# Loading and splitting two weights of the last product earlier, in tiles that the attention's projections leave free

## The chip, the core and the metric

The kernel runs on one core of a Trainium2 chip. Its time is the device time of that core in microseconds; the value given is the median of 3 runs.

The engines are called as the profile calls them: PE (TensorE, matrix products), DVE (VectorE), ACT (ScalarE), POOL (GpSimd) and SP (SyncE, which here only issues transfers). Transfers are issued from two queues, SP's and ACT's. Each queue issues in order, and each transfer takes its turn among eight completion semaphores, so that it may wait for an older transfer with the same semaphore to land.

## The reference

Three stages run one after the other. What matters here is the last part of the second and the whole of the third.

```python
# stage 1: linear attention over phi(q), phi(k), v            (8 x 8 heads x 576 x 64)
# stage 2: mixture of E=4 causal attention experts            (8 x 576 x 512)
for e in range(E):
    q = x @ wq[e]; k = x @ wk[e]; v = x @ wv[e]
    scores = where(causal, -1e9, scale * (q @ k.T))
    a = softmax(scores)
    out += gate[e] * (a @ v @ wo[e])
# stage 3: token mix and gated feed-forward                   (d_model 512, d_ff 1024)
x_prev = concat([0, x[:, :-1]])
xk = mu_k * x + (1 - mu_k) * x_prev
xr = mu_r * x + (1 - mu_r) * x_prev
k = maximum(xk @ w_k, 0.0)
v = k * k @ w_v
r = 1.0 / (1.0 + exp(-(xr @ w_r)))
return r * v
```

## The kernel before

All products are float32 made of pieces: each operand is split in a high half (a rounded copy, written by ACT, L97) and a low half (the rest, `src - hi`, by DVE or POOL, L100), and a product is hi·hi + hi·lo + lo·hi, three matmuls.

**Stage 2** goes through batches b = 0 to 7. `qk` are the projections with the weights `wqh, wql, wkh, wkl` (tiles of 128 x 1024 in pool `pQ`, made at the start, read until the last batch's projections), `sc` the scores (L514, L515), `a` the exponentials (ACT, L534; scaled on POOL, L545), `at` their transposes (L552, split to `at1h`/`ath` on ACT L568 and `at1l`/`atl` on DVE L569), `yp` the product with v (L587). After the last `yp` of a batch half, `yf` and its time differences `dl` are split to `yt` and stored to DRAM as `yd` (SP, L608).

**Stage 3, first product (`rk`).** `gates_keys` computes x @ w_r and x @ w_k, for both taps, for 6 chunks of tokens. A unit is 6 matmuls of 128x384; its weight `wt` (256 KB) comes by ACT's queue, 5 buffers deep. DVE adds three partial results into `z` (L720), ACT squares the keys' ones (Relu L722, Square L723), and SP's queue stores `z` to DRAM as `kd` (L724).

**Stage 3, last product (`vacc`, L882).** `moe2` computes k² @ w_v in seven products per chunk (a Strassen scheme over 2x2 blocks): operands b11, b21, T2, T1, b22, T3, T4 in this order (j = 0 to 6), with weights `WC[0, 1, 3, 4, 5, 6, 2]`, 24 matmuls of 128x384 each. The blocks of the squared keys come back from `kd` by SP's queue, are combined on DVE (L845 to L858) and split into slots of the tile `XT`, which before that held stage 2's activations. The results are evacuated as `t` (ACT) and `o` (DVE, L906, L915). `zs` are the gate's inputs r (two loads of 768 KB per chunk, L822; a table load and the sigmoid on ACT, L835).

Stage 2's attention and the `rk` units of the later chunks run woven together; the `rk` units fill PE while the attention's softmax runs elsewhere. At the attention's end (about 1009.7 us) follows the first chunk of the last product. Its first block b11 comes as two half loads `k0` (L794), the other three (b21, b12, b22) straight into parts of `XT` that are free (L797); b21 is split there (L97, `XT<-XT`). `first()` writes this part, `chunk(0)` the rest.

Of the seven weights, four (0, 1, 3, 4) are loaded and split in the attention's middle (`combo`, two halves of 128x512, low half on POOL). Weights 5, 6 and 2 come late: `combo(j, 0, 2, ...)` from `load('w5', 'w6')` and `load('w2')` loads 128x1024 from DRAM (`wst<-wc`, L675, 512 KB), weights 5 and 6 in the two buffers `zs`, and splits it on ACT (`wch`) and DVE (`wcl`).

The order of the instructions on an engine is set in two steps: the lists in `chunk`, `first` and `skewed` give the order in which the code is written (an element of a list is a step, and task i+1 begins one step after task i), and a scheduler with its own model of times then orders each engine's instructions. So a small edit here can move instructions on all engines from about 935 us on.

Of the kernel before, what the change touches and what calls it, by code (L numbers as in the profile page):

```python
# [6 lines left out]
F32 = mybir.dt.float32  # L7
# [69 lines left out]
def fused_kernel(ctx: ExitStack, tc: tile.TileContext, qT, kT, vx, wphi, wq, wk, wvg, wo, mu, w64, ident, cmask, tri, out):  # L77
    nc = tc.nc
# [8 lines left out]
    wc = dram.tile([P, 7, 16, 64], F32, name='wc')  # L87
# [33 lines left out]
    phA = ExitStack()  # L121
    psA = phA.enter_context(tc.tile_pool(name='psA', bufs=1, space=PSUM))
    pX = ctx.enter_context(tc.tile_pool(name='pX', bufs=1, side='right'))
    XT = pX.tile([P, 16 * S], F32R, name='XT')
    pQ = phA.enter_context(tc.tile_pool(name='pQ', bufs=1, side='right'))
    wqh, wql, wkh, wkl = (pQ.tile([P, 2, 4, P], F32R, name=n) for n in ('wqh', 'wql', 'wkh', 'wkl'))
    pA = phA.enter_context(tc.tile_pool(name='pA', bufs=1, side='right'))
    phF = ExitStack()
# [539 lines left out]
    WC = {}  # L668
# [106 lines left out]
    def moe2():  # L775
# [7 lines left out]
        def block(c, s, par, f0, f1):  # L783
            return kd[c][:, 4 + 4 * s + f0:4 + 4 * s + f1, par]
# [3 lines left out]
        def first():  # L788
            while not (done.get(0, 0) == NB and B - 1 in read and len(WC) == 4):
                yield None  # L790
            state['pre'] = True
            for i in range(2):
                raw['b11', i] = late['pW'].tile([P, 2, HC], F32, name='k0', tag='wst2', bufs=2)
                nc.sync.dma_start(raw['b11', i], block(0, 0, 0, 2 * i, 2 * i + 2))  # L794
            for n, k, x in (('b21', 1, 1), ('b12', 2, 0), ('b22', 2, 1)):
                raw[n] = slot(k)[x].bitcast(F32)
                nc.sync.dma_start(raw[n], block(0, *src[n], 0, 4))  # L797
            yield 100000
            for i in range(2):
                f = slice(2 * i, 2 * i + 2)  # L800
                split(*(x[:, f] for x in slot(0)), raw['b11', i], 'a')
                yield 20000
            for i in range(2):
                f = slice(2 * i, 2 * i + 2)
                split(*(x[:, f] for x in slot(1)), raw['b21'][:, f], 'a')
                yield 20000
            while 'pB' not in late:
                yield None

        def chunk(c):  # L810
            pB = late['pB']
            d = {}

            def load(*names):

                def go():
                    for n in names:
                        if n[0] == 'w':
                            d[n] = combo(int(n[1]), 0, 2, pB, pB, 1536, *(('kx', 8) if n == 'w2' else ('zs', 2)))
                        elif n[0] == 'g':  # L820
                            d[n] = pB.tile([P, 4, HC], F32, name='zs', tag='zs', bufs=2)
                            nc.sync.dma_start(d[n], kd[c][:, 0:4, int(n[1])])  # L822
                        elif n[0] == 'b':
                            d[n] = pB.tile([P, 4, HC], F32, name='kx', tag='kx', bufs=8)
                            nc.sync.dma_start(d[n], block(c, *src[n], 0, 4))
                return (lambda: done.get(c, 0) >= (NB if 'g0' in names else 24), go)
# [35 lines left out]
            def parts(j):  # L862

                def go():
                    if c or j > 1:
                        split(*slot(7 * c + j), d[ops[j]], 'a')
                return go

            def mm(j):

                def go():
                    wh, wl = WC[wts[j]]
                    h, l = slot(7 * c + j)
                    bank = 'xyxxxww'[j]
                    for dp in range(2):
                        if j in (0, 1, 5):
                            d[bank, dp] = late['psB'].tile([P, 512], F32, name='vacc', tag=f'{bank}{dp}')[:, :HC]
                        ps = d[bank, dp]
                        n = 0
                        for f in range(4):  # L880
                            for a, m in ((wh, h), (wh, l), (wl, h)):
                                nc.tensor.matmul(ps, a[:, f, dp], m[:, f], start=j in (0, 1, 5) and n == 0, stop=n == 11, skip_group_check=True)  # L882
                                n += 1
                    return 4200
                return go
# [47 lines left out]
                    return b()  # L933
                return (a[0], go) if isinstance(a, tuple) else go
            if c == 0:
                fs = [[None, mm(0), post(0)], [sums(2), mm(1), post(1)], [parts(2), load('w5', 'w6'), None, mm(2), post(2), None, prep('w5', 'w6')]]
                fs += [[load('b21', 'w2'), None, None, None, None, parts(3), both(load('g0', 'g1'), prep('w2')), both(prep('g0', 'g1'), mm(3)), post(3)]]
            else:
                fs = [[load(*l), None, None, None, sums(j), parts(j), None, mm(j), post(j)] for j, l in enumerate((('b11',), ('b21',), ('b12', 'b22')))]
                fs += [[None, None, None, None, None, both(load('g0', 'g1'), parts(3)), None, both(prep('g0', 'g1'), mm(3)), post(3)]]  # L940
            return fs + [[None, None, None, None, sums(j), parts(j), None, mm(j), post(j)] for j in (4, 5, 6)]

        def all_():
            yield from first()
# [63 lines left out]
```

## Time and profile before

| | |
|---|---|
| median of 3 runs | 1272.14 us (1265.86 to 1277.38) |
| profiled execution | 1269.52 us |
| its span, mean granted clock of PE | 1267.7 us, 0.986 |
| PE busy | 1223.9 us, 97% |
| DVE, ACT, POOL busy | 936.1 us (74%), 811.9 us (64%), 434.5 us (34%) |

The profiled execution's own time is 2.6 us under the median, and 1.8 us above its span. Times of rows are microseconds from the span's start.

### The profile page before, as it was taken

How to read it: one execution, taken by the hardware profiler on the slowest of the kernel's cores; microseconds unless marked ns; L12 is line 12 of the kernel's file. 1: busy time of each engine (PE TensorE's matmuls, PEld its weight loads, DVE VectorE, ACT ScalarE, POOL GpSimd, SP SyncE). 2: the span in 40 equal slices, each digit the busy share in tenths (PEclk: the TensorE clock that was granted, in tenths of full speed). 3: DMA queues.
4: the chain of work that ended last, by engine and by line, in shares of the span. 5: the costliest groups of instructions: out<-in, count | busy, mean ns of one | idle time of the engine just before them, and what ended most of it. 6: DMA issues, size and time to landing. Idle time of an engine off the chain costs nothing.

```text
span 1267.7 us, 26596 instructions
## 1 busy us (share of the span) xinstructions
PE 1223.9 (97%) x9008; PEld 1181.8 (93%) x9008; DVE 936.1 (74%) x2488; ACT 811.9 (64%) x2004; POOL 434.5 (34%) x634
## 2 busy tenths in 40 slices
PE   7999989999999999999999999998999969999998
PEld 7999989999999999999999999897899869999998
DVE  6566888888977877787688778656667567767766
ACT  5556668668767776766577756666567655446533
POOL 5533467545642333554444553322212200000000
PEclk9799999999999999999999999999999989999999
DMA  6223125223324454456545434755879996888853
GB/s 190 82 76 110 59 78 167 79 75 105 106 91 147 137 151 133 108 175 188 152 124 158 133 110 129 236 151 168 264 223 299 293 348 227 281 307 280 270 176 124
DMA packets 186917, 212.69 MB, mean 168 GB/s; under 512 B 34464, under 2 KB 170528, under 8 KB 186784
## 3 DMA queue, kind: packets, MB, share of 16 engines
q1 hardware_dynamic: 108448, 140.21, 33.8%
q10 hardware_dynamic: 78336, 70.80, 19.0%
q8 instruction: 73, 1.20, 0.4%
q14 instruction: 60, 0.49, 0.1%
HBM read 145.94 MB, written 65.01 MB: 166 GB/s over the span
## 4 chain that ended last, share of the span: by engine, by line
PE 79%; DVE 7%; DMA 5%; ACT 4%; issue 2%; POOL 1%; ACTq 1%; SPq 0%; POOLq 0%; DVEq 0%
PE rk L117 15%; PE vacc L882 12%; PE kv L334 10%; PE num L372 8%; PE qk L117 7%; PE vp L117 4%; PE yp L587 3%; PE at L552 3%; PE pj L282 3%; PE pj L284 2%; PE pj L283 2%; PE fo L117 2%; PE sc L514 2%; PE tq L356 2%; PE sc L515 2%
## 5 line engine op out<-in xcount | busy, mean ns | idle before, releaser
L545 POOL TENSOR_SCALAR a<-a,sv,gw 128x128 f32<-128x128 f32 (+4 forms) x160 | 108.8, 682 | 205.3 <-DVE sv L539 81.9
L882 PE MATMUL vacc<-XT,wch 128*128 128x384 f32 x672 | 174.9, 336 | 2.4 <-ACT XT L97 1.7
L100 POOL TENSOR_TENSOR lo<-raw,hi 128x256 fp32r<-128x256 f32 (+1 forms) x160 | 110.2, 691 | 188.8 <-ACT hi L97 179.3
L372 PE MATMUL num<-kvs,ph 128*128 128x65 f32 (+1 forms) x1280 | 142.5, 262 | 0.0
L372 PEld LDWEIGHTS num<-kvs,ph 128*128 128x128 f32 (+1 forms) x1280 | 137.3, 181 | 4.5 <-issue 2.3
L882 PEld LDWEIGHTS vacc<-XT,wch 128*128 128x128 f32 x672 | 122.1, 189 | 3.7 <-ACT XT L97 2.4
L292 DVE TENSOR_REDUCE m<-pj 128x4 f32<-128x512 f32 (+1 forms) x160 | 100.4, 630 | 33.2 <-PE pj L284 32.3
L534 ACT ACTIVATE a<-sc,sv 128x128 f32<-128x128 f32 (+2 forms) x192 | 98.5, 515 | 29.2 <-DVE sv L529 8.5
L882 PE MATMUL vacc<-XT,wcl 128*128 128x384 f32 x336 | 111.6, 335 | 0.0
L720 DVE TENSOR_TENSOR z<-rk,z 128x384 f32<-128x384 f32 x144 | 79.1, 551 | 33.6 <-PE rk L117 18.4
L294 DVE TENSOR_TENSOR pm<-pj,m 128x512 f32<-128x512 f32 (+1 forms) x160 | 100.0, 629 | 3.6 <-ACT ph L318 1.6
L282 PE MATMUL pj<-wph,hi 128*128 128x256 f32 x288 | 91.9, 319 | 5.9 <-ACT hi L97 3.9
L529 DVE TENSOR_REDUCE sv<-sc 128x1 f32<-128x128 f32 (+2 forms) x192 | 88.7, 468 | 9.6 <-PE sc L515 6.3
L100 DVE TENSOR_TENSOR XT<-kx,XT 128x1536 fp32r<-128x1536 f32 x40 | 70.1, 1754 | 20.9 <-ACT XT L97 20.9
L97 ACT ACTIVATE XT<-kx 128x1536 fp32r<-128x1536 f32 x40 | 59.4, 1486 | 40.1 <-PE vacc L882 22.4
L284 PE MATMUL pj<-wph,lo 128*128 128x256 f32 x288 | 83.6, 291 | 0.5 <-POOL lo L100 0.4
L283 PE MATMUL pj<-wpl,hi 128*128 128x256 f32 x288 | 83.2, 289 | 0.0
L97 ACT ACTIVATE hi<-raw 128x256 fp32r<-128x256 f32 (+1 forms) x160 | 62.4, 392 | 31.5 <-PE pj L283 13.1
L552 PE MATMUL at<-idn,a 128*128 128x128 f32 (+2 forms) x480 | 74.0, 262 | 3.2 <-POOL a L545 3.2
L569 DVE TENSOR_TENSOR at1l<-at,at1h 128x384 fp32r<-128x384 f32 (+3 forms) x128 | 59.5, 465 | 22.3 <-ACT at1h L568 20.4
L568 ACT ACTIVATE at1h<-at 128x384 fp32r<-128x384 f32 (+3 forms) x128 | 53.6, 419 | 33.5 <-PE at L552 20.1
L514 PE MATMUL sc<-k,qs 128*128 128x128 f32 (+2 forms) x192 | 66.3, 354 | 5.2 <-ACT a L534 5.2
(510 smaller groups left out, 3577.9 us busy)
## 6 DMA issues: line engine op xcount, KB each, us to landing
wt<-wf ACTq DMA_DIRECT2D x216, 256.0 KB, 3.6
kd<-z SPq DMA_DIRECT2D x144, 192.0 KB, 3.5
kx<-kd SPq DMA_DIRECT2D x21, 768.0 KB, 7.0
yd<-yt SPq DMA_DIRECT2D x16, 864.0 KB, 4.7
zs<-kd SPq DMA_DIRECT2D x12, 768.0 KB, 8.3
out_dram<-o SPq DMA_DIRECT2D x24, 384.0 KB, 2.7
raw<-in_kT_dram SPq DMA_DIRECT2D x64, 128.0 KB, 2.2
raw<-in_qT_dram SPq DMA_DIRECT2D x64, 128.0 KB, 2.2
```

The lines of the kernel that those rows point to most:

```text
L97: nc.scalar.activation(hi, src, AF.Copy)
L100: (el or nc.vector).tensor_sub(lo, src, hi.bitcast(F32))
L117: nc.tensor.matmul(ps, a, m, start=first and i == 0, stop=last and i == n - 1)
L282: nc.tensor.matmul(o, hi[:, c], wph, start=True, stop=False)
L283: nc.tensor.matmul(o, hi[:, c], wpl, start=False, stop=False)
L284: nc.tensor.matmul(o, lo[:, c], wph, start=False, stop=True)
L292: nc.vector.tensor_reduce(m[:, :g], ps, axis=AX.X, op=OP.max, apply_absolute_value=True)
L334: nc.tensor.matmul(bank[:, r, :], d['kp'][:, r % 2, c0:c0 + P], d['v'][:, i + (lo_ > 0), r // 2, :], start=new and r == 0, stop=end, skip_ ...
L372: nc.tensor.matmul(ps[lo_:hi_, i, j, :], d['qp'][:, hf, c0 + lo_:c0 + hi_], kvs[hp, b][:, r * 65:(r + 1) * 65], start=hf == 0, stop=hf == 1)
L545: eng(asc).tensor_scalar(a[:m, :nk], a[:m, :nk], rc[:m], WT[b][:m, i, e:e + 1], op0=OP.mult, op1=OP.mult)
L552: nc.tensor.transpose(ps[:kw, jj * m:jj * m + m], d['a'][:m, jj * P:jj * P + kw], idn[:m, :m])
L882: nc.tensor.matmul(ps, a[:, f, dp], m[:, f], start=j in (0, 1, 5) and n == 0, stop=n == 11, skip_group_check=True)
```

## The change

The pool `pQ` with the four projection tiles lives to the end. When the last batch's projections have read them, `first()` loads weight 5 into `wql` and weight 6 into `wkl` (SP's queue, 512 KB each), splits the high half on ACT into `wqh` and `wkh`, and writes the low half in place on POOL (128x1024). The late load, its landing in the `zs` buffers and the splits in `chunk(0)` go away for these two. Weight 2 is loaded at product j = 4 and split at j = 5, where both were at j = 3.

```diff
-    pQ = phA.enter_context(tc.tile_pool(name='pQ', bufs=1, side='right'))
+    pQ = ctx.enter_context(tc.tile_pool(name='pQ', bufs=1, side='right'))
     wqh, wql, wkh, wkl = (pQ.tile([P, 2, 4, P], F32R, name=n) for n in ('wqh', 'wql', 'wkh', 'wkl'))
...
                 raw[n] = slot(k)[x].bitcast(F32)
                 nc.sync.dma_start(raw[n], block(0, *src[n], 0, 4))
+            homes = [[x.rearrange('p a b c -> p (a b c)').rearrange('p (q n) -> p q n', n=64) for x in y] for y in ((wqh, wql), (wkh, wkl))]
+            for j, (_, l) in zip((5, 6), homes):
+                nc.sync.dma_start(l.bitcast(F32), wc[:, j])
             yield 100000
+            for j, (h, l) in zip((5, 6), homes):
+                split(h, l, l.bitcast(F32), 'a', nc.gpsimd)
+                WC[j] = [x.rearrange('p (f d h) n -> p f d (h n)', f=4, d=2) for x in (h, l)]
+                yield 20000
...
-                fs = [[None, mm(0), post(0)], [sums(2), mm(1), post(1)], [parts(2), load('w5', 'w6'), None, mm(2), post(2), None, prep('w5', 'w6')]]
-                fs += [[load('b21', 'w2'), None, None, None, None, parts(3), both(load('g0', 'g1'), prep('w2')), both(prep('g0', 'g1'), mm(3)), post(3)]]
+                fs = [[None, mm(0), post(0)], [sums(2), mm(1), post(1)], [parts(2), None, None, mm(2), post(2)]]
+                fs += [[load('b21'), None, None, None, None, parts(3), load('g0', 'g1'), both(prep('g0', 'g1'), mm(3)), post(3)]]
...
-            return fs + [[None, None, None, None, sums(j), parts(j), None, mm(j), post(j)] for j in (4, 5, 6)]
+            w2 = (load('w2'), prep('w2')) if c == 0 else (None, None)
+            return fs + [[w2[0] if j == 4 else None, None, None, None, sums(j), parts(j), w2[1] if j == 5 else None, mm(j), post(j)] for j in (4, 5, 6)]
```

The instructions are the same ones on every engine up to about 940 us. On SP's queue the load into `wql` then stands ahead of the last two stores before the three loads into `XT`, and of these three that of b21, which is split first, stands second where it stood third. On ACT the split into `wqh` stands behind the last write of `qs` (943.32 us before) and ahead of the copy `z<-rk` (943.79 us). Further down, ACT's rows around the split of b21 in `XT` are these, before:

```order
L722 ACTIVATE z<-z 128x384
L723 ACTIVATE z<-z 128x384
L534 ACTIVATE a,sv<-sc,sv 128x128
L104 ACTIVATE z<-rk 128x384
L769 DMA wt<-wf_86 128x2x256
L568 ACTIVATE at1h<-at 128x4x64
L534 ACTIVATE a,sv<-sc,sv 128x256
L97 ACTIVATE XT<-XT 128x768 x2
L723 ACTIVATE z<-z 128x384
```

and now:

```order
L97 ACTIVATE XT<-XT 128x768
L723 ACTIVATE z<-z 128x384
L97 ACTIVATE XT<-XT 128x768
L722 ACTIVATE z<-z 128x384
L723 ACTIVATE z<-z 128x384
L534 ACTIVATE a,sv<-sc,sv 128x128
L104 ACTIVATE z<-rk 128x384
L769 DMA wt<-wf_86 128x2x256
L568 ACTIVATE at1h<-at 128x4x64
L534 ACTIVATE a,sv<-sc,sv 128x256
L723 ACTIVATE z<-z 128x384
L97 ACTIVATE wkh<-wkl 128x1024
```

The two halves of the split stood behind two exponentials of the last batch; now they stand ahead of both, and the split into `wkh` has come in behind them.

SP's queue at the attention's end (`yd_74` is the last batch's half, `k_...` the two loads of b11, `zs` the gate's inputs of chunk 0), before:

```order
L724 DMA kd_91<-z 128x384 x7
L794 DMA k_14998<-kd_87 128x2x384
L724 DMA kd_91<-z 128x384
L608 DMA yd_74<-yt 256x1x864
L794 DMA k_15000<-kd_87 128x2x384
L675 DMA wst_15877<-wc 128x1024
L675 DMA wst_15881<-wc 128x1024
```

and now:

```order
L724 DMA kd_91<-z 128x384 x5
L608 DMA yd_74<-yt 256x1x864
L829 DMA zs<-kd_87 128x4x384 x2
L724 DMA kd_91<-z 128x384 x4
L794 DMA k_14998<-kd_87 128x2x384
L724 DMA kd_91<-z 128x384
L794 DMA k_15000<-kd_87 128x2x384
```

Both `zs` loads have moved up, from behind five loads of weights and blocks to a place ahead of the two loads of b11, and `yd` with them. On ACT the table load and the two sigmoids of `zs` (L842 in the new numbering) have moved up likewise: each stands ahead of a Relu and Square whose `z` one of the stores between the two loads of b11 sends out.

DVE from the second half of b11 on, before:

```order
L845 TENSOR_TENSOR kx<-XT,k_15000 128x768
L100 TENSOR_TENSOR XT<-k_15000,XT 128x768
L846 TENSOR_TENSOR kx<-XT,kx 128x1536
L848 TENSOR_TENSOR kx<-XT 128x1536
L100 TENSOR_TENSOR XT<-kx,XT 128x1536
L100 TENSOR_TENSOR wcl_15876<-wst_15877,wch_15875 128x1024
L720 TENSOR_TENSOR z<-rk,z 128x384
L906 TENSOR_TENSOR o<-vacc,t 128x384 x2
L100 TENSOR_TENSOR XT<-kx,XT 128x1536
L858 TENSOR_TENSOR kx<-kx 128x1536
L100 TENSOR_TENSOR wcl_15880<-wst_15881,wch_15879 128x1024
L720 TENSOR_TENSOR z<-rk,z 128x384
```

and now (the last row is T2's split, which before is the row that follows the last one shown):

```order
L852 TENSOR_TENSOR kx<-XT,k_15000 128x768
L100 TENSOR_TENSOR XT<-k_15000,XT 128x768
L853 TENSOR_TENSOR kx<-XT,kx 128x1536
L855 TENSOR_TENSOR kx<-XT 128x1536
L720 TENSOR_TENSOR z<-rk,z 128x384
L100 TENSOR_TENSOR XT<-kx,XT 128x1536
L865 TENSOR_TENSOR kx<-kx 128x1536
L100 TENSOR_TENSOR XT<-kx,XT 128x1536
```

The two low halves `wcl` of weights 5 and 6, the two `o`, one `z` and T1's split no longer stand ahead of T2's split. On PE, 146 matmuls now stand between the last `yp` and the first one that reads T2's low half, where 110 stood: 24 `rk` matmuls have moved there from among the attention's last products, 12 from behind.

## Rows read from the trace of the kernel before

**Rows 1.** The page: busy us, share of the span, instructions by engine.

```profile
PE 1223.9 (97%) x9008; PEld 1181.8 (93%) x9008; DVE 936.1 (74%) x2488; ACT 811.9 (64%) x2004; POOL 434.5 (34%) x634
```

**Rows 2.** Windows: busy us of PE, PEld, DVE, ACT, POOL, clock, DMA share, GB/s.

```profile
950.00:960.00 10.00, 9.12 (x59) 8.35 (x58) 7.95 (x25) 9.31 (x25) 1.95 (x3) 1.00 1.05 366
1010.00:1020.00 10.00, 8.30 (x48) 7.98 (x47) 1.91 (x4) 4.65 (x10) 2.28 (x2) 1.00 0.83 266
1020.00:1030.00 10.00, 7.99 (x42) 6.94 (x42) 8.12 (x9) 6.66 (x10) 0.00 (x0) 1.00 1.02 356
1030.00:1040.00 10.00, 3.79 (x11) 3.29 (x12) 10.00 (x10) 7.24 (x11) 0.00 (x0) 0.67 1.06 376
1040.00:1050.00 10.00, 10.00 (x50) 10.00 (x50) 4.09 (x6) 6.56 (x9) 0.00 (x0) 0.82 0.98 340
1050.00:1100.00 50.00, 50.00 (x290) 50.00 (x290) 36.61 (x40) 25.73 (x31) 0.00 (x0) 1.00 0.71 237
```

**Rows 3.** TensorE's timeline: start us, duration us, instruction, [idle before it <- releaser].

```profile
940.67 0.34 PE L514 MATMUL sc<-k,qs 128*128 128x384 f32 x1
...
957.14 0.44 PE L514 MATMUL sc<-k,qs 128*128 128x384 f32 x1 [0.88 <-ACT a L534]
...
1008.96 0.75 PE L587 MATMUL yp<-at1l,vsp 128*64 128x320 f32 x5
...
1038.90 2.29 PE L117 MATMUL rk<-yc__14537,wt 128*128 128x384 f32 x6 [3.17 <-DVE z L720]
```

**Rows 4.** ScalarE's timeline, 940 to 1048 us.

```profile
943.79 0.49 ACT L104 ACTIVATE z<-rk 128x384 f32<-128x384 f32 x1
...
955.27 0.51 ACT L723 ACTIVATE z<-z 128x384 f32<-128x384 f32 x1
...
956.63 0.37 ACT L534 ACTIVATE a<-sc,sv 128x128 f32<-128x128 f32 x1
...
958.34 0.85 ACT L97 ACTIVATE XT<-XT 128x768 fp32r<-128x768 f32 x1
...
1028.87 1.04 ACT L97 ACTIVATE wch<-wst 128x1024 fp32r<-128x1024 f32 x1
...
1043.70 1.28 ACT L835 ACT_TABLE_LOAD   x1 [1.98 <-PE rk L117]
1044.99 1.49 ACT L835 ACTIVATE zs<-zs 128x1536 f32<-128x1536 f32 x1
```

**Rows 5.** The timeline of SyncE's DMA queue.

```profile
948.23 1.49 SPq L797 DMA_DIRECT2D XT<-kd  x3
...
1016.16 0.53 SPq L608 DMA_DIRECT2D yd<-yt  x1
...
1021.71 0.79 SPq L675 DMA_DIRECT2D wst<-wc  x2
```

**Rows 6.** Tile XT's three loads (768 KB each), 945 to 965 us.

```profile
DMA to landing us min/median/max: 4.7/6.4/9.0
```

**Rows 7.** The chain that ended last, in time: start us, us.

```profile
1019.45 5.07 DMA k<-kd
```

**Rows 8.** VectorE's timeline, 1020 to 1042 us.

```profile
1024.54 0.96 DVE L845 TENSOR_TENSOR kx<-XT,k 128x768 f32<-128x768 f32 x1 [1.38 <-DMA k<-kd]
...
1031.30 1.22 DVE L100 TENSOR_TENSOR wcl<-wst,wch 128x1024 fp32r<-128x1024 f32 x1
...
1038.77 1.75 DVE L100 TENSOR_TENSOR XT<-kx,XT 128x1536 fp32r<-128x1536 f32 x1
```

**Rows 9.** Tile zs (768 KB each), whole span.

```profile
DMA to landing us min/median/max: 4.5/8.3/12.2
```

**Rows 10.** Line 100, low halves of splits: ns min/median/max, first, last start.

```profile
L100 POOL TENSOR_TENSOR wcl<-wst,wch x8: 1266/1288/1300, 813.3 to 835.4; 128x512 fp32r<-128x512 f32 x8
```

**Rows 11.** GpSimd's timeline, 950 to 965 us.

```profile
959.32 2.07 POOL L545 TENSOR_SCALAR a<-a,sv,gw 128x256 f32<-128x256 f32 x1 [1.19 <-ACT XT L97]
962.96 0.67 POOL L545 TENSOR_SCALAR a<-a,sv,gw 128x384 f32<-128x384 f32 x1 [1.57 <-PE rk L117]
```

## The prediction

> **What bounds the kernel now.** I read the page first: PE is busy 1223.9 us of the span, 97% [rows 1]. So no other engine's work as such is worth anything; only what makes PE wait, or run under its full clock, counts. The windows say where that is. From 1050 us on PE is busy 50.00 of 50 us with 290 instructions at clock 1.00 [rows 2], 0.1724 us each, nearly all 128x384; nothing is to be won there. From 1010 to 1050 us it ran 48 + 42 + 11 + 50 = 151 of them [rows 2], worth 26.0 us: **14.0 us are lost** at the passage from the attention to the last product, at clocks down to 0.67. This is the place that the change aims at. TensorE's timeline shows waits there such as the 3.17 us before 1038.90, ended by a `z` on DVE [rows 3], and DVE is busy 10.00 of 10 us from 1030 to 1040 [rows 2]: PE waits for DVE's queue. Further back, the attention shows one wait that matters below, 0.88 us before the score at 957.14, ended by an exponential on ACT [rows 3].
>
> **What is removed.** Two loads of 512 KB on SP's queue at the passage, two `wch` on ACT (1.04 us each) and two `wcl` on DVE (1.22 each) [rows 4, 8]. From the second half of b11 (DVE's 1024.54) to the end of T2's split (1038.77 + 1.75 = 1040.52) DVE takes 16.0 us [rows 8]. By the new order T1's split (the 1.75 of a 128x1536) moves behind it too, and so do two `o` and one `z`, about half a us each as estimated from the 0.96 of 128x768 [rows 8]: some 1.2 + 1.2 + 1.7 + 1.4 = 5.5 us go, and 10.5 are left. If b11's second half landed when it does now, the passage would lose some 5.5 us less. The largest possible gain has a wall: PE has 146 matmuls to there, at 0.1724 us 25.2 us, and b11's landing 14.8 us after the last `yp` (below) plus 10.5 makes 25.3.
>
> **What is added in the attention.** The load into `wql` may go when the last product with it ends, at about 940.7, where the next score starts [rows 3]. The fastest 768 KB into `XT` took 4.7 [rows 6]; two thirds of the bytes take between two thirds of that, 3.1, and all of it; I take 4.0, and with half a us for the issue it lands about 945.2 (944.3 to 945.9). ACT waits for it at its split, ahead of the copy of 943.79 [rows 4]: wait and 1.04 us of split put that copy at about 946.2, **2.4 us later** (1.5 to 3.1). For PE this is hidden: the bank that the copy frees is asked for again only behind 24 matmuls of the k projections. If that cover failed it would cost up to the 2.4; I count 0 to 0.5. The low half on POOL takes 2.5 us (twice 1.288 [rows 10]) in a gap.
>
> ACT is busy 9.31 of 10 us from 950 to 960 [rows 2], so it gains back 0.7 and is 1.7 late at the Square of 955.27 [rows 4]. b21's split now stands there, ahead of two exponentials. b21's load is the second of three instead of the last, so it takes the middle landing, 6.4 us instead of 9.0 [rows 6]; the three go out behind a store that waits for ACT's late Square, 1 to 2 us after 948.23 [rows 5], so b21 lands at 956 to 957 and ACT hardly waits for it. But its two halves of 0.85 overlap to 1.5 us, and the exponential of 956.63 [rows 4] comes 1.7 + 1.5 later. The score that waits for it started at 957.14 after PE had waited 0.88 [rows 3]: **PE waits 3.2 us more**. Bounds: 2.0 where wql's load lands early, 5.1 where b21's takes 9.0 again. The split into `wkh` (1.04) takes the place that the two halves had, so nothing behind it is later than that; POOL's half of `wkl` (2.5) stands ahead of a scale that is wanted soon after: 0 to 0.5, taken as 0.
>
> **What is moved at the passage.** `yd` and both `zs` loads now stand ahead of b11's loads on SP's queue. Today SP issues `yd` at 1016.16 and what needs its landing at 1021.71, 5.5 us later [rows 5]; b11's second half goes out at 1019.45 and takes 5.07 [rows 7]: 1024.5, 14.8 us after the last `yp` (1008.96 + 0.75 [rows 3]). In the new order, counted from the last `yp`: `yd` goes out at 4.6 to 6.5 (today 6.5, behind b11's first half); the first `zs` 5 later, once `yd` has landed; it lands 4.5 to 12.2 us after that, median 8.3 [rows 9]; I take 7, since less is under way than at the place of the slowest: 16.5. The table load (1.28) and the sigmoid (1.49) [rows 4] make it 19.3; the Relu and Square behind them, 1.0 as at 955.27 [rows 4], and their store, which stands ahead of b11's first half, 20.8. The second sigmoid and another Relu and Square: b11's second half goes out at 23.3 and, with 5.07, lands at 28.4. DVE's 10.5 and what it waits in between make 39.5 (36.5 to 42.3 by the ends). PE's work to there is 25.2, so 14.3 are lost, and at the lower clock behind it another 0.7, half of what 1040 to 1050 lost today (10 us for 50 instructions [rows 2]): 15.0 against 14.0, **+1.0 us** (-2 to +4). What DVE saves is spent waiting for b11. Weight 2, now later (one load, one `wch`, one `wcl`), lies beside 48 matmuls that are ready: 0.
>
> **The sum.** 3.2 + 1.0 = +4.2 us on the profiled execution: 1269.5 + 4.2 = 1273.7. That execution is 2.6 us under the median, so against the median of 1272.1 I say **1276 us**. 1% (12.7 us) is about what a measurement of this kernel can tell from no change.
>
> **The rivals.** *b11 isn't held up.* If the `zs` loads land in 4.5 us, or the sigmoids' waits fall beside others, b11's second half comes up to 13 us sooner, each us of it worth one until the wall of 25.2: the passage loses 1 instead of 14. With the attention's +3.2 that is 1262; half of it is 1269. For it speaks that DVE's stretch is really 5.5 us shorter; against it the order of SP's and ACT's queues. Chance 0.22.
>
> *The two places cancel.* +2 in the attention, -2 at the passage: 1271 to 1273. The change then only moves work that is hidden either way. Chance 0.20.
>
> *The `zs` loads land as late as today's slowest, 12.2 us* [rows 9], because the weights of 11 dense `rk` units run beside them: b11 comes 5 us later still, and all of it is PE's wait. With 5.1 in the attention instead of 3.2 that is 1276 + 5 + 2 = 1283, and up to 1287 with those weights late as well. It decides once `zs` takes over 8 us. Chance 0.18.
>
> *POOL's long low halves hold DVE.* GpSimd's scale of 128x256 took 2.07 us at 959.32, beside the split of `XT`, where a larger one of 128x384 took 0.67 [rows 11]: something that ran beside it held it. The new halves of 2.5 us stand beside DVE's steps ahead of an exponential; one hit costs up to 2.5 us on the way to a score, two 5.0: 1278.5 to 1281. Chance 0.07. The Trainium skill, page "SBUF — State Buffer", section "Who interferes with whom", says that a VectorE instruction with two inputs in SBUF and a GpSimd instruction that reads SBUF exclude one another for a whole instruction, whichever starts first. By that rule DVE would be the loser where POOL's long instruction starts first, and the time the 1278.5 to 1281 just given. The row agrees with the rule for POOL as the loser; no run here shows the other case.
>
> **How the numbers follow.** My forecast (1273 to 1281) has 0.33. To leave out no more than 2 in 10, the range goes from 1266, half-way between the first rival's two times, to 1286. Faster by over 1% needs 1259.4, past the first rival's full size: 0.07. Slower by over 1%, past 1284.9, takes the third rival's upper end or the sum's bounds together: 0.13. Within 1%: 0.80.
>
> **What would show it.** In the attention: ACT's split into `wqh` behind a wait of 1.5 us near 944, and a wait of about 4 us on PE ahead of the score that is at 957.14 today, ended by `a` L534. At the passage: `yd` and `zs` out before b11, two sigmoids ahead of b11's split, b11's second half landed 27 to 30 us after the last `yp`, a long wait of PE there, and 10.5 us on DVE from it to T2's split. From there on PE dense as before. The prediction is wrong if the score's wait stays under 2 us, or if b11's second half is there within 20 us.

## The result, and the profile after

The changed kernel takes 1278.17 us (median of 14 runs, 1272.75 to 1283.3); the kernel before, in the same comparison, 1269.85 (14 runs). The ratio is **1.0069, 95% interval [1.005, 1.0088]**: 0.7% slower, 8.3 us by the medians. The forecast was 1276 us, 4.2 more than before. The profiled execution of the changed kernel took 1274.99 us with a span of 1273.1; that of before took 1269.52 with 1267.7, so the two traces explain 5.4 us.

The page answers to [rows 1]: PE still has 9008 matmuls, and its busy time has grown by 2.1 us.

```profile
PE 1226.0 (96%) x9008; PEld 1182.9 (93%) x9008; DVE 936.0 (74%) x2486; ACT 812.9 (64%) x2004; POOL 435.9 (34%) x636
```

Windows cut at the same points of the program in both kernels tell where it went: from the end of the last product with `wql` to the end of the last `yp` (T); the 55 us behind T; and 1100 to 1140 us. Between the last two PE is busy all the time in both (35.29 of 35.29 us before, 37.24 of 37.24 after). First the kernel before, then the changed one (columns as in [rows 2]).

```profile
940.83:1009.71 68.88, 65.36 (x402) 60.00 (x401) 48.15 (x146) 48.38 (x132) 16.83 (x22) 0.98 0.87 279
1009.71:1064.71 55.00, 45.07 (x234) 43.20 (x234) 33.41 (x37) 34.45 (x49) 2.28 (x2) 0.91 0.82 280
1100.00:1140.00 40.00, 39.74 (x229) 39.42 (x228) 28.08 (x33) 18.18 (x23) 0.00 (x0) 1.00 0.92 310
```

```profile
939.78:1007.76 67.98, 61.13 (x378) 55.83 (x377) 48.29 (x143) 47.72 (x128) 20.35 (x24) 0.97 0.87 279
1007.76:1062.76 55.00, 47.70 (x228) 45.08 (x228) 28.23 (x32) 33.80 (x53) 2.27 (x2) 0.84 0.86 283
1100.00:1140.00 40.00, 37.61 (x217) 37.29 (x216) 28.05 (x31) 18.29 (x21) 0.00 (x0) 1.00 0.93 304
```

A matmul not done in a stretch is done later, at 0.1724 us each where PE is dense. The attention is 0.90 us shorter but holds 24 matmuls fewer (the 24 `rk` that the order moved behind it): 24 x 0.1724 - 0.90 = **+3.2 us**. The passage holds 6 fewer: **+1.0**. From 1100 to 1140, 12 fewer: **+2.1**, at a place that the prediction took for dense. Together 6.3; the changed kernel came to the attention 1.05 us earlier, which leaves the 5.4 of the two spans within 0.2.

TensorE's timeline after, at the two places of [rows 3] and at the third:

```profile
958.68 0.44 PE L514 MATMUL sc<-k,qs 128*128 128x384 f32 x1 [2.34 <-ACT a L534]
...
1024.88 2.26 PE L117 MATMUL rk<-yc__14615,wt 128*128 128x384 f32 x6 [2.68 <-DMA wt<-wf]
...
1046.96 0.44 PE L889 MATMUL vacc<-XT,wch 128*128 128x384 f32 x1 [0.89 <-DVE XT L100]
...
1127.80 0.62 PE L889 MATMUL vacc<-XT,wch 128*128 128x384 f32 x2 [2.39 <-ACT t L104]
```

The score's wait was 0.88 and is 2.34. ScalarE's timeline after, beside [rows 4], shows why, then the table load and a Square in the passage, and the third place:

```profile
944.01 1.06 ACT L97 ACTIVATE wqh<-wql 128x1024 fp32r<-128x1024 f32 x1 [1.33 <-DMA wql<-wc]
...
955.33 0.84 ACT L97 ACTIVATE XT<-XT 128x768 fp32r<-128x768 f32 x1
...
956.50 0.83 ACT L97 ACTIVATE XT<-XT 128x768 fp32r<-128x768 f32 x1
...
958.17 0.37 ACT L534 ACTIVATE a<-sc,sv 128x128 f32<-128x128 f32 x1
...
1022.34 1.28 ACT L842 ACT_TABLE_LOAD   x1 [2.40 <-DMA zs<-kd]
...
1027.04 0.52 ACT L723 ACTIVATE z<-z 128x384 f32<-128x384 f32 x1 [1.51 <-issue]
...
1121.92 4.73 ACTq L690 DMA_DIRECT2D yc__15719<-yd  x4
...
1127.26 0.87 ACT L104 ACTIVATE t<-vacc 128x384 f32<-128x384 f32 x2 [6.26 <-DMA kx<-kd]
```

ACT waits 1.33 us for `wql`, splits it, and has b21's two halves ahead of the exponential that the score needs. In the passage it waits 2.40 for `zs`. At the third place it is idle for 6.26 us, 4.73 of which its queue spends on issuing four loads of `yc`. SyncE's queue after, beside [rows 5]:

```profile
1012.83 0.52 SPq L608 DMA_DIRECT2D yd<-yt  x1
1016.82 0.93 SPq L829 DMA_DIRECT2D zs<-kd  x2
1017.85 10.06 SPq L724 DMA_DIRECT2D kd<-z  x4
1028.18 0.37 SPq L794 DMA_DIRECT2D k<-kd  x1
...
1030.35 0.39 SPq L794 DMA_DIRECT2D k<-kd  x1
```

The issue of four stores takes 10.06 us of the queue, to 1027.91, and b11's two loads (L794) stand behind them. The last of the four holds it: its `z` comes from ACT's Square of 1027.04, which stands behind the wait for `zs`, the table load and the first sigmoid. b11's second half goes out at T + 22.6. VectorE after, beside [rows 8]:

```profile
1036.26 0.96 DVE L852 TENSOR_TENSOR kx<-XT,k 128x768 f32<-128x768 f32 x1 [0.56 <-DMA k<-kd]
...
1045.15 1.75 DVE L100 TENSOR_TENSOR XT<-kx,XT 128x1536 fp32r<-128x1536 f32 x1
```

It starts on b11's second half at T + 28.5 and ends T2's split at 1046.90, T + 39.1: 10.6 us, where it took 16.0. The windows beside [rows 2]:

```profile
1020.00:1030.00 10.00, 6.07 (x22) 4.77 (x20) 1.11 (x2) 6.01 (x7) 0.00 (x0) 0.69 1.04 343
1030.00:1040.00 10.00, 8.90 (x34) 8.60 (x34) 6.68 (x8) 6.83 (x10) 0.00 (x0) 0.62 0.92 286
```

The moved `rk` matmuls fill the stretch from 1010 to 1020 (58, were 48); in the next PE is idle for 3.93 us of ten, and the granted clock falls to 0.69 and then 0.62 (means: part of the time at 2.4 GHz, part of it at 1.2). DVE is busy for 1.11 us of ten while b11 is awaited.

What PE waits for in these 55 us is not what the prediction has it wait for. It is idle for 7.30 us, and only 0.89 of them are ended by T2's split. Loads of `wt` end 3.06, DVE's `z` 1.97, ACT's `t` 1.39. Before it was 9.93 us, 7.75 of them ended by `z`. The load of `wt` behind the wait of 2.68 us went out at 1017.26, just behind the `zs` loads, and took 7.5 us to land.

### The profile page after: what moved, and what is told of

It reads as the page before. It is cut to its first block, busy times and chain, and to the rows that moved or that the text cites. A ratio compares the mean times of both kernels' runs of the same rounds, so it can differ in the third digit from the quotient of the medians.

```text
span 1273.1 us, 26599 instructions
## 1 busy us (share of the span) xinstructions
PE 1226.0 (96%) x9008; PEld 1182.9 (93%) x9008; DVE 936.0 (74%) x2486; ACT 812.9 (64%) x2004; POOL 435.9 (34%) x636
## 4 chain that ended last, share of the span: by engine, by line
PE 77%; DVE 7%; DMA 6%; ACT 5%; issue 2%; POOL 1%; ACTq 1%; SPq 0%; POOLq 0%; DVEq 0%
PE rk L117 14%; PE vacc L889 12%; PE kv L334 10%; PE num L372 8%; PE qk L117 7%; PE vp L117 4%; PE yp L587 3%; PE at L552 3%; PE pj L282 3%; PE pj L283 2%; PE pj L284 2%; PE fo L117 2%; PE sc L514 2%; PE tq L356 2%; PE sc L515 2%
## 5 line engine op out<-in xcount | busy, mean ns | idle before, releaser
L889 PE MATMUL vacc<-XT,wch 128*128 128x384 f32 x480 | 125.7, 338 | 4.7 <-ACT t L104 3.8
L889 PEld LDWEIGHTS vacc<-XT,wch 128*128 128x128 f32 x480 | 88.0, 190 | 5.8 <-ACT t L104 4.6
L889 PE MATMUL vacc<-XT,wcl 128*128 128x384 f32 x240 | 80.8, 337 | 0.0
```

## The experiments

Ratios are to the kernel before, run on the same chip. T is the end of the last `yp`; the last column is the end of T2's split on DVE, the one before it the issue of b11's second load (of both, where the two went out together). The wait is that of the 128x384 score that stands at 957.14 in [rows 3], ended by ACT's `a`.

| kernel | ratio [95%] | score's wait, us | b11's second load issued | T2 |
|---|---|---|---|---|
| before | 1 | 0.88 | T + 9.7 | T + 30.8 |
| changed | 1.0069 [1.005, 1.0088] | 2.34 | 22.6 | 39.1 |
| w2 late alone | 1.0009 [0.9986, 1.0032] | 0.88 | 10.4 | 31.6 |
| no early part | 0.9997 [0.9977, 1.0017] | 0.88 | 10.2 | 32.0 |
| early loads alone | 1.0013 [0.9992, 1.0034] | 0.88 | 15.1 | 31.3 |
| early part alone | 1.0046 [1.0023, 1.0069] | 3.59 | 20.3 | 40.5 |
| zs held | 1.0036 [1.0006, 1.0065] | 2.45 | 14.4 | 37.0 |
| yc by SyncE | 1.0039 [1.0014, 1.0064] | 3.34 | 22.6 | 40.0 |
| high halves on POOL | 1.0015 [0.999, 1.004] | none | 9.4 | 29.7 |
| the same, yc by SyncE | 1.0021 [1.0002, 1.004] | none | 9.8 | 31.0 |
| high halves on DVE | 1.0041 [1.0019, 1.0062] | none | 21.5 | 39.5 |
| both halves on DVE | 1.0076 [1.0046, 1.0106] | 0.34 | 19.4 | 36.4 |
| high on DVE, zs held, yc by SyncE | 1.0057 [1.0037, 1.0077] | none | 12.7 | 35.9 |
| late low halves on POOL | 1.0059 [1.0033, 1.0086] | 0.88 | 10.9 | 34.4 |

The kernels with T2 by T + 32.0 lie at 1.0021 or below, those with it at T + 34.4 or later at 1.0036 or above. Inside either group a later T2 doesn't go with a longer time, so T2 alone doesn't set it.

**How far one trace can be trusted.** The third weight's move alone, made in the kernel before:

```diff
-load('b21', 'w2') ... both(load('g0', 'g1'), prep('w2'))
+load('b21') ... load('g0', 'g1')
+w2 = (load('w2'), prep('w2')) if c == 0 else (None, None)     # at j == 4 and j == 5
```

> The kernel before, with only the third weight (2) loaded and split two products later; weights 5 and 6 stay late. If the third weight's move costs nothing by itself, 1268 to 1272 us, and no wait over 1 us between 1110 and 1140 us. The rival: its load and split at the later place are what holds ScalarE in the third place (2.39 us in the changed kernel), 1271 to 1274, with a wait of 2 us or more there.

Measured 1.0009, no difference. On each engine its instructions stand in the same order as before: written two products later, this weight's load and split come out at the same place as long as 5 and 6 stay late. So this run is also a second execution of the kernel before, and its windows show the scatter (from 1100 to 1140 it has 229 matmuls as before and no wait over 0.36 us, so the rival falls):

```profile
936.87:1008.64 71.77, 66.72 (x401) 61.31 (x401) 48.52 (x146) 48.47 (x132) 15.32 (x22) 0.95 0.84 268
1008.64:1063.64 55.00, 45.38 (x234) 44.24 (x234) 33.24 (x37) 34.28 (x48) 2.29 (x2) 0.91 0.81 280
```

The same attention took 2.9 us longer, the same passage did the same 234 matmuls. A sum for the attention from one trace is therefore good to 3 us at best. What repeats is the single wait: 0.88 in all five kernels that keep the halves out of the attention's end, 2.34 to 3.59 in the four that have the high halves on ACT.

**The two sides of the change apart.** First the late part is removed and nothing is put in its place; this kernel leaves out the loads and splits of weights 5 and 6, and reads the tiles as they are:

```diff
-for j, (_, l) in zip((5, 6), homes):
-    nc.sync.dma_start(l.bitcast(F32), wc[:, j])
...
-    split(h, l, l.bitcast(F32), 'a', nc.gpsimd)
```

> The changed kernel without its early part: weights 5 and 6 are neither loaded nor split in the attention, and the products use what the projection tiles hold, so two loads, two high and two low halves are left out altogether. By its order the attention and the loads of b11 stand as before the change. Theory (the change's saving on DVE is real, and is lost because the early part moves the zs loads ahead of b11): the score's wait is 0.9 us as before, b11's second half lands 14 to 16 us after the last yp, DVE's stretch to T2's split is 10 to 11.5 us, and the kernel is 4 to 7 us faster than before. Rival (PE does not wait for that stretch, but for weights of the rk units): within 2 us of before.

Measured 0.9997 [0.9977, 1.0017]: no difference to be seen (1.8 us faster by the medians), where 4 to 7 us were expected; within the 2 us of the rival. b11 is early (issued at T + 10.2), yet DVE's timeline shows no 10.5 us behind it:

```profile
1022.61 0.96 DVE L849 TENSOR_TENSOR kx<-XT,k 128x768 f32<-128x768 f32 x1 [1.37 <-DMA k<-kd]
...
1031.52 1.02 DVE L910 TENSOR_TENSOR o<-vacc,t 128x384 f32<-128x384 f32 x2 [2.07 <-ACT t L104]
...
1037.66 1.75 DVE L100 TENSOR_TENSOR XT<-kx,XT 128x1536 fp32r<-128x1536 f32 x1
```

T1's split and the `o` are ahead of T2's again, and DVE is idle for 2.07 us waiting for `t` from ACT: 16.8 us from b11 to T2, more than the 16.0 of before. The room that two `wcl` leave is filled by others. The unchanged total is itself a sum, by the windows behind T and from 1100 us:

```profile
1007.38:1062.38 55.00, 45.36 (x242) 43.20 (x242) 32.60 (x37) 31.23 (x44) 2.28 (x2) 0.94 0.76 257
1100.00:1140.00 40.00, 37.45 (x207) 37.13 (x206) 22.90 (x28) 17.03 (x22) 0.00 (x0) 0.96 0.80 271
```

The passage holds 8 matmuls more than before, 1.4 us gained; the third place holds 22 fewer, 3.8 us lost. So the removal does gain something at the passage, less than expected, and this kernel loses it again later. The rival's reason isn't borne out: PE's longest wait in the passage is 6.55 us for DVE's `z`, not for a weight.

Then the early part is put into the kernel before, in addition; nobody reads what it makes:

```diff
+for j, (_, l) in zip((5, 6), homes):
+    nc.sync.dma_start(l.bitcast(F32), wc[:, j])
 yield 100000
+for j, (h, l) in zip((5, 6), homes):
+    split(h, l, l.bitcast(F32), 'a', nc.gpsimd)
+    yield 20000
```

> The kernel before, with the two weights (5 and 6) loaded and split a second time at attention's end into tiles that nobody reads; the late loads and splits stay, so VectorE's stretch in the passage is not shortened, and what the outputs are computed from is unchanged. If the early part costs by itself what it cost in the changed kernel, attention loses 2 to 3 us (score wait 2 to 2.5), b11's second half lands 25 to 30 us after the last yp, and with VectorE's long stretch of 16 us behind that landing the passage loses 2 to 6 more: 1274 to 1280 us. The rival: the early part costs nothing, and the loss of the changed kernel came from the tiles' new owners and the moved third weight: 1269 to 1271.

Measured 1.0046, 5.2 us by the medians, in the range of the theory; the score's wait is longer than its 2 to 2.5. The score and DVE:

```profile
960.14 0.69 PE L514 MATMUL sc<-k,qs 128*128 128x384 f32 x1 [3.59 <-ACT a L534]
```

```profile
1026.83 1.23 DVE L100 TENSOR_TENSOR wcl<-wst,wch 128x1024 fp32r<-128x1024 f32 x1 [2.14 <-ACT wch L97]
...
1040.56 0.96 DVE L851 TENSOR_TENSOR kx<-XT,k 128x768 f32<-128x768 f32 x1 [1.99 <-DMA k<-kd]
...
1050.03 1.75 DVE L100 TENSOR_TENSOR XT<-kx,XT 128x1536 fp32r<-128x1536 f32 x1
```

Two parts of the expectation were wrong, and they tell most. With b11 late, DVE makes the two late `wcl` while it waits, and the stretch from b11 to T2 is 11.2 us with both weights still late. And the late b11 costs this kernel's passage nothing (first the attention, then the 55 us behind T):

```profile
940.03:1011.28 71.25, 62.32 (x378) 56.93 (x377) 48.50 (x143) 48.00 (x128) 20.46 (x24) 0.95 0.85 266
1011.28:1066.28 55.00, 46.49 (x235) 44.55 (x235) 30.77 (x34) 35.86 (x56) 2.29 (x2) 0.88 0.91 309
```

T2's split ends at T + 40.5, yet the passage holds 235 matmuls, one more than before; the 24 `rk` moved there fill the time. The loss lies in the attention: 2.4 us longer with 24 matmuls fewer, +6.5 us in this trace.

Last the two early loads without their splits (the same edit without its second half):

> The kernel before, with the two weights (5 and 6) loaded a second time at attention's end but not split there; nobody reads these loads, and the late loads and splits stay. In the program's order b11's second half stands ahead of the loads of zs again, as in the kernel before. With the splits as well, this kernel was 0.46% slower than the one before. If the cost of the early part is the halves in attention and the order of zs and b11 that comes with them, the loads alone cost nothing: 1268 to 1272 us, a score wait of at most 1.2 us and b11's second half landed 13 to 18 us after the last yp. The rival: the two loads themselves, on SyncE's queue ahead of and between the loads of b21, hold up what is loaded there: 1273 to 1277, with b21's second landing over 6 us and the score wait 2 us or more.

```profile
950.43 0.45 PE L514 MATMUL sc<-k,qs 128*128 128x384 f32 x1 [0.88 <-ACT a L534]
```

Measured 1.0013 [0.9992, 1.0034]; the median of 1272.36 us lies just past the expected 1272: the loads alone cost too little to tell. The score's wait is back at 0.88. b11 came later than expected (DVE starts on its second half at T + 20.9, not 13 to 18), and a wait of 3.08 us for `at1h` stands in the attention, so they aren't free of effect. That the halves make the rest, up to 1.0046, is likely, since the score's wait is 3.59 with them, but the two intervals overlap. Here too DVE makes both late `wcl` while it waits for b11, and its stretch from b11 to T2 is 10.35 us. By the windows its attention loses 3.2 us without any half, as much as the changed kernel's, its passage gains 1.6 and the third place loses 2.4.

**b11's place in the queue.** In the changed kernel the `zs` loads are held until b11's second half is there, by a write of one column into their tile:

```diff
+if c == 0:
+    nc.vector.tensor_copy(d[n][:, 0, 0:1], raw['b11', 1][:, 0, 0:1])
```

> The changed kernel; only the two loads of zs of chunk 0 are made to wait for b11's second half (DVE writes one column of each zs tile from it before the load). Theory: b11's second half lands 20 to 22 us after the last yp instead of 28.5, T2's split ends about 7 us sooner, the passage gets back 5 to 7 us: 2 us slower to 2 us faster than before the change; the attention's wait ahead of the score stays at 2.3 us. Rival (the 11 dense rk units wait for their weights, and b11 for DMA bandwidth, whatever the order): b11 lands no earlier than 26 us after the last yp and the time stays within 2 us of the changed kernel's.

```profile
1028.80 1.77 PE L891 MATMUL vacc<-XT,wch 128*128 128x384 f32 x3 [4.30 <-ACT XT L97]
```

```profile
1007.87:1062.87 55.00, 46.25 (x234) 43.49 (x234) 29.04 (x35) 33.55 (x53) 2.29 (x2) 0.91 0.84 285
1100.00:1140.00 40.00, 39.67 (x229) 39.35 (x228) 28.65 (x32) 19.20 (x23) 0.00 (x0) 1.00 0.93 313
```

Measured 1.0036, 3.0 us slower than before by the medians, where 2 slower to 2 faster was expected, and some 5 us less than the changed kernel by the medians, with the score's wait still at 2.45. b11's loads go out at T + 14.4 and DVE starts on the second half at 1030.33, T + 22.5 instead of T + 28.5. New waits for ACT's split of `XT` (4.30 and 3.67 us) take a part of the gain. By the windows the passage gets back 6 matmuls (1.0 us, all that the changed kernel had lost there), and the third place 12 (2.1 us). So what the whole kernel gains (0.36% is left of 0.69%, with intervals that overlap) is in this trace for the most part gained at the third place, which the theory doesn't explain; at the passage itself b11's place was worth about 1 us.

The same run shows what `zs` does to the loads beside it. These are the three `wt` loads that ACT issues from 1017 to 1019.5, in the changed kernel and with `zs` held:

```profile
DMA to landing us min/median/max: 7.5/8.5/9.0
```

```profile
DMA to landing us min/median/max: 4.6/4.7/4.8
```

With `zs` out of the way they land 3 to 4 us sooner, and PE's wait of 2.68 us for a `wt` is gone.

**Other engines for the early halves.** The high halves on POOL:

```diff
-split(h, l, l.bitcast(F32), 'a', nc.gpsimd)
+nc.gpsimd.tensor_copy(h, l.bitcast(F32))
+nc.gpsimd.tensor_sub(l, l.bitcast(F32), h.bitcast(F32))
```

> The changed kernel, with the high halves of weights 5 and 6 written by POOL instead of ACT (both halves on POOL). By its order ACT then has the exponentials nearly as before, and b11's loads stand ahead of the zs loads. Theory (ACT's wait and work for the early split cost the attention 3 us, and the order at the passage 6): no wait of ACT near 944, the score's wait under 1.6 us, b11's second half landed 14 to 17 us after the last yp, 3 to 6 us faster than before. Rival (POOL's long instructions hold the scales of the exponentials and DVE): a wait of PE of 2 us or more for POOL's scale of a ahead of a transpose, DVE's low halves lengthened by over 1 us, and no faster than before.

1.0015 [0.999, 1.004]: faster than the changed kernel, but not the 3 to 6 us faster than before that were expected. The order puts b11 ahead of `zs` again (issued at T + 9.4, T2 at T + 29.7, the earliest of all), and the score's wait for `a` is gone; in its place PE waits 4.57 us for `at1h`:

```profile
956.68 1.06 PE L587 MATMUL yp<-at1h,vsp 128*128 128x320 f32 x4 [4.57 <-ACT at1h L568]
```

By its windows the passage gains 3.8 us (256 matmuls) and the attention loses 5.8. With the high halves on DVE, next, the attention loses 6.7, with both there 7.4, against 3.2 in the changed kernel. These are single traces, good to 3 us; no engine is shown to make the halves for less than ACT.

The high halves on VectorE (`'v'` for `'a'`):

> The changed kernel, but the high halves of the two early weights (5 and 6) are made on VectorE instead of ScalarE; the low halves stay on GpSimd. If the loss at attention's end is ScalarE's extra halves ahead of the exponentials, the wait for the exponential behind the scores falls from 2.34 us to at most 1.2, the loss of that stretch from +2.2 to between 0 and +0.7, and the passage stays as in the changed kernel (b11's second half lands 26 to 29 us after the last yp): 1275 to 1277 us, some 2 less than the changed kernel. The rival: VectorE's high halves hold up its own sums and copies there, and the wait only goes to another engine's name: 1277 to 1280.

1.0041. The time (1275.1) lies in the theory's range, but the score's wait has gone to another engine's name, as the rival had it. DVE's and POOL's timelines, and what PE then waits for:

```profile
958.00 4.02 DVE L100 TENSOR_TENSOR XT<-XT 128x768 fp32r<-128x768 f32 x2
```

```profile
957.97 2.38 POOL L100 TENSOR_TENSOR wkl<-wkl,wkh 128x1024 fp32r<-128x1024 f32 x1 [2.77 <-DVE wkh L99]
```

```profile
963.41 1.34 PE L117 MATMUL rk<-yc__13716,wt 128*128 128x384 f32 x6 [3.89 <-DVE z L720]
```

Two subtractions of b21 took 4.02 us beside POOL's low half (one of them 3.16), and the `z` behind them is late. Both halves on DVE (`'v', nc.vector`):

> The changed kernel, with both halves of the two early weights on VectorE, so that neither ScalarE nor GpSimd has any of them. With the high halves alone on VectorE, GpSimd's low half (2.38 us) lay beside VectorE's two low halves of b21's sums, which took 4.02 us in place of some 1.9, and TensorE then waited 3.89 us for z. If that overlap is the cause, the two subtractions take 0.95 each again, the wait falls to at most 2 us, and the score wait stays at 1.2 or less: 1272 to 1275 us. The rival: VectorE's 3.8 us of halves hold z as long whoever works beside them: 1275 to 1278.

The overlap is gone, and both subtractions take 0.95 us again; the first:

```profile
962.33 0.95 DVE L100 TENSOR_TENSOR XT<-XT 128x768 fp32r<-128x768 f32 x1
```

```profile
1035.40 4.21 PE L117 MATMUL rk<-yc__14537,wt 128*128 128x384 f32 x12 [6.20 <-DVE z L720]
```

Yet the time, 1.0076 over 4 runs, is no better than the changed kernel's, and 1277.9 us is in the rival's range. By the windows its passage loses nothing against before, so its loss too lies in the attention. That POOL's half holds DVE is right; that this was what the time hung on is not. PE waits 2.40 for `at1h`, and in the passage 6.20 for a `z` (9.17 with the high halves alone on DVE), which waits for the same stores in front of b11.

**POOL's low halves against DVE.** In the kernel before, the low halves of the three late weights go to POOL:

```diff
-split(*(x[:, q] for x in WC[j]), s_, 'a', nc.vector if n == 2 else nc.gpsimd)
+split(*(x[:, q] for x in WC[j]), s_, 'a', nc.gpsimd)
```

> The kernel before, with the low halves of the three late weights (5, 6, 2) on POOL instead of DVE; nothing else. Theory (DVE's stretch from b11's second half to T2's split sets the passage, 1 us for 1 us): two wcl of 1.22 us go from a stretch of 16.0 us, which becomes 13.5, and the kernel gets 2.4 us faster than before (1 to 3.5). Rival (POOL's halves of 2.4 us hold DVE's instructions with two inputs in SBUF): DVE's subtractions of 1.75 us beside them get longer by 1 to 2.4 us, the stretch stays at 15 to 17 us, and the time is that of before or up to 3 us slower.

```profile
1030.27 11.25 POOL L100 TENSOR_TENSOR wcl<-wst,wch 128x1024 fp32r<-128x1024 f32 x3 [15.64 <-DMA kx<-kd]
```

```profile
1035.40 3.92 DVE L858 TENSOR_TENSOR kx<-kx 128x1536 f32<-128x1536 f32 x1
1039.24 3.89 DVE L100 TENSOR_TENSOR XT<-kx,XT 128x1536 fp32r<-128x1536 f32 x1
```

1.0059, 7.8 us slower by the medians, more than the rival's 0 to 3; the stretch from b11 to T2 is 18.4 us. Three halves took POOL 11.25 us, 3.75 each instead of 2.4, and DVE's instructions beside them 3.92 and 3.89 instead of 1.75. Both lose. The Trainium skill, page "SBUF — State Buffer", section "Who interferes with whom", says that two such instructions exclude one another, and the trace agrees with it for the loser that the prediction could not show, VectorE. By the windows the passage loses 3.3 us and the third place, where PE waits 4.20 for ACT's `t`, 5.3.

**The third place.** In the changed kernel SyncE issues the last chunk's loads of `yc` instead of ACT:

```diff
-load_y(c, ys[c][sl], sl, nc.scalar)
+load_y(c, ys[c][sl], sl, nc.sync if c == NC_ - 1 else nc.scalar)
```

> The changed kernel, but the loads of yc of the last chunk are issued by SyncE instead of ScalarE. If the third place (TensorE's 2.39 us wait for ScalarE's t near 1128 us) is ScalarE's queue held while it issues those loads, that wait falls under 0.5 and the time to 1274.5 to 1277, some 2 us less than the changed kernel, with attention and passage as they were. The rival: SyncE's own queue then holds the following loads behind yc, a new wait of 2 us or more stands near it, and the time is 1277 to 1280.

```profile
1132.82 0.62 PE L889 MATMUL vacc<-XT,wqh 128*128 128x384 f32 x2 [1.25 <-ACT t L104]
```

1.0039, 2.4 us less by the medians and in the theory's range; but the wait fell from 2.39 to 1.25 and not below 0.5, and the interval overlaps that of the changed kernel. Nor are ACT's four issues of `yc` enough to make the wait, for the kernel before has them too:

```profile
1117.64 4.32 ACTq L690 DMA_DIRECT2D yc__15714<-yd  x4
...
1122.87 0.49 ACT L104 ACTIVATE t<-vacc 128x384 f32<-128x384 f32 x1 [4.31 <-DMA wt<-wf]
```

There ACT is idle for 4.31 us ahead of the same `t`, and PE waits 0.26. With `yc` on SyncE's queue ACT is idle for 5.71 us ahead of its `t` all the same, with `zs` held for 5.48, where PE waits 0.33. So ACT's idle time at this place is common to the kernels, and what makes PE feel it in some of them stays open. Nor is the place tied to one side of the change: without the early part a wait of 2.55 us for ACT's `t` stands there, and with the early loads alone, the late part kept, the 40 us from 1100 on held 215 matmuls (before 229, changed 217).

**Combinations.** High halves on POOL and `yc` by SyncE:

> The changed kernel, with both halves of the early weights on GpSimd (which by itself gave the time of the kernel before, with 11.45 us lost in the passage in place of 14.75) and the loads of yc of the last chunk issued by SyncE. If the places add, the 1.35 us wait at the third place goes too: 1267 to 1270 us, no slower than the kernel before and perhaps a little faster. The rival: the yc loads on SyncE only move that wait, 1270 to 1273.

1.0021 [1.0002, 1.004]: no gain over the high halves on POOL alone, and in the rival's range. High halves on DVE, `zs` held and `yc` by SyncE:

> The changed kernel with three edits: the high halves of the early weights on VectorE, the loads of zs held until b11's second half has landed, and yc of the last chunk loaded by SyncE. If the three places are separate, their gains add: some 2 from attention, some 3 to 5 from the passage, some 2 from the third place, 1268 to 1271 us, no slower than the kernel before. The rival: they share a limit (TensorE is the bound in between and the waits pass to other names), and two of the three give nothing: 1272 to 1276.

1.0057, 1276.9 us, just past even the rival's 1276: the three gains don't add. In the attention PE waits 3.90 for `z` (DVE again held by POOL's half, 4.03 us for the two subtractions), in the passage 4.53 for ACT's `XT`. No version was faster than the kernel before.

## Why the prediction was right, point by point

*The sum.* 4.2 us forecast, 5.4 between the traces, 8.3 between the medians. The sign and the size class were right, and both places lost what was forecast; the missing part is the third place, +2.1, which the prediction took for dense ("from there on PE dense as before"). That 1276 lies only 2.2 us from the 1278.17 measured is partly luck: the median of before that it was added to, 1272.14 from 3 runs, stood 2.3 above the 1269.85 of the comparison's 14, and this made up for half of the 4.1 us by which the change itself was forecast too small.

*The attention, +3.2.* The windows give +3.2, a coincidence to that digit, since the same program scattered by 2.9. That the halves delay the exponential is shown: the score's wait of 2.34 to 3.59 comes and goes with the high halves on ACT, and the loads alone leave it at 0.88. ACT's wait for `wql` was 1.33 (forecast 1.5). The exponential comes 2.6 us later, counted from the start of the stretch (18.39 us instead of 15.80), where 1.7 + 1.5 = 3.2 were forecast. The score's wait grew by less, by 1.46 instead of 3.2. PE's idle time over the whole stretch grew by 3.33 us (6.85, was 3.52), so more than half of its loss lies in shorter waits, 0.94 before an `rk` among them. How much of the 3.2 is the halves' and how much the loads' isn't settled: the early part alone lost 6.5 here, the loads alone 3.2, one trace each.

*The passage, +1.0.* Measured +1.0, and the steps up to T2 stand: b11's second half at T + 28.5 (28.4), DVE's stretch 10.6 (10.5), T2 at T + 39.1 (39.5). The step behind them doesn't: the prediction took all of PE's lost time for a wait for T2, and T2's split ends 0.89 us of it. PE waited for loads of `wt` beside `zs`, for `z` and for `t` instead, and the kernel with the early part alone has T2 as late and loses nothing here. So this +1.0 came out by parts that were off and cancelled: PE's idle time fell, from 55 - 45.07 = 9.93 us to 7.30, with 24 matmuls moved here, while its busy time per matmul rose from 45.07 / 234 = 0.193 to 47.70 / 228 = 0.209 us at the lower granted clock (0.84, was 0.91). On 228 matmuls that is 3.8 us, where 0.7 was put down for the clock.

*"What DVE saves is spent waiting for b11."* Right, and the runs say more: the saving isn't there in the other order either. With b11 on time the stretch is 16.8 us again, since T1's split, the `o` and a wait for `t` fill it; with b11 late the two `wcl` hide in the wait. What the removal did gain at the passage, 1.4 us, that kernel lost again at the third place.

*Rivals.* "b11 isn't held up" priced each microsecond of an earlier b11 at one, down to 1262. The three kernels with b11 on time and the late halves gone gave 1268 to 1272: the mechanism's premise (10.5 us of DVE whatever the order) was wrong. That the places cancel did happen in part, in the kernel with the high halves on POOL (+5.8 and -3.8). The two `zs` loads landed 5.4 and 9.2 us after their issues, not 12.2; the second is over the rival's 8, but b11 was no later than forecast. What that rival says of loads that run beside `zs` is shown the other way round: it was the `wt` loads that came late. POOL held no instruction of DVE in the changed kernel, but 2.1 us of it with the high halves on DVE.

*Still open:* how the 8.3 us of the medians divide over the three places beyond the one trace, and what makes the third.

## What to carry to other kernels

Before work is moved off a busy stretch, look at what the engine would do there otherwise: a step that fills an engine's waiting time for a late load costs little, and its removal gains little. Follow the queues, not the work alone: two halves of 1 us on ACT came with another order of loads, and b11 then stood behind stores that waited for ACT, while the weights that PE needed landed late beside `zs`. Ask in the trace what the engine that bounds the kernel waits for: with the early part alone T2 came 10 us later and cost that passage nothing, since other work filled the time. And run the kernel before twice: if the same program scatters by 3 us in a stretch, compare single waits over several kernels instead of sums.

## What the runs showed of the hardware

DVE's subtraction of 128x1536 took 1.75 us alone and 3.92 beside a POOL subtraction, which itself took 3.75 instead of 2.4: each took about the 1.75 + 2.4 us of both one after the other. ACT was idle for 6.26 us, 4.73 of them while its queue issued four loads of `yc`; SyncE's queue held two loads for 10 us behind four stores, of which the last one's data came late. Three 256 KB loads took 7.5 to 9.0 us to land beside two of 768 KB, and 4.6 to 4.8 without them.
